# Router logits of an attention + FFN + mixture kernel: x tiles as the stationary operand instead of the gate

## The chip, the cores and the metric

The kernel runs on one NeuronCore of a Trainium2 chip, in one launch. The metric is the device time of one execution in microseconds. Three executions of the kernel before took 2273.41, 2275.58 and 2281.95 us; the median is 2275.58 us.

TensorE (PE in the profile; PEld is its weight load) does the matrix products: a stationary operand (`lhsT`) is loaded, then the columns of a moving operand (`rhs`) are streamed past it, and the result lands in PSUM. VectorE is DVE, ScalarE is ACT, GpSimd is POOL. SyncE (SP) issues all DMAs of this kernel.

## What is computed

Three layers follow one another on 4 sequences of 576 tokens, 2304 tokens in all, width 512: causal attention with a decay, a gated FFN, and a mixture of 8 experts whose weights per token come from a router. The change is in the router:

```python
def _moe2_ref(x, w_gate, w1, w2):
    logits = x @ w_gate                      # 2304 x 512 by 512 x 8
    logits = logits - logits.max()
    P = np.exp(logits)
    for _ in range(8):                       # rows and columns normalised in turn
        P /= P.sum(1, keepdims=True) + 1e-09
        P /= P.sum(0, keepdims=True) + 1e-09
        P *= N / E
    for e in range(E):
        out += P[:, e:e+1] * (np.maximum(x @ w1[e], 0) @ w2[e])
```

## The kernel before, in words

**Precision.** Products are made from split operands: every fp32 value is cast to fp32r (`hi`, on ACT) and the rest `x - hi` is formed on POOL (`rest`, L142). Most products take three matmuls: hi·hi, hi·lo and lo·hi.

**Stages.** `merge` interleaves two streams of steps by their costs: the attention of sequence b (`attn_unit(b)`) with the FFN of sequence b-1 (`moe_unit(b-1)`). The FFN leaves its result `x` of 512 x 576 with the *features* on the 128 partitions (four chunks k) and the tokens along the row. Sequence 3's FFN has no attention beside it (L519). Then come two phases of 32 slices (256 hidden columns of one expert): `wload` fetches and splits the weights, `eup` makes the hidden values of two sequences with seven products in place of eight (Strassen, L578), `edown` multiplies by w2 for nine tiles of 128 tokens and adds into `acc`. Expert 0 of phase 0 is added unweighted, since the router's weights are not there yet; from expert 1 on, each tile is scaled by `lg[:, t, e]` (L626, L630).

**The router.** At the end of each sequence's FFN, `finish` (L433) writes x to DRAM, and for each half of 288 tokens and each pair i of feature chunks casts x to `f` (ACT, L443, POOL for the rest), and runs four matmuls (L447) with the gate stationary and 288 tokens moving. The gate tile `gw` holds, for each feature chunk, 8 columns of hi, 8 of lo and 112 of zeros, so each product has 128 output rows, of which 16 count. ACT copies these 16 rows (L451) and a DMA writes them to `lgd` in DRAM (L452). In phase 0, after the first slice, `gate` (L637) reads `lgd` back in five pieces, transposes each tile of 16 x 128 on TensorE (L645), and DVE adds the lo part to the hi part into `lg`, with tokens on the partitions (L648, L649). `balance` (L651) then makes the exponentials and eight rounds of row and column sums on DVE, with one small matmul a round (L674).

**What sets the order.** The Tile framework puts instructions on each engine in an order that its scheduler chooses, and adds the semaphore waits; each engine then runs its own list strictly in that order. PSUM has eight banks: `ps_m` has three tiles of one bank each, for the FFN's products and for `pl`; when it is closed (L520), its banks go to later pools, `ps_y` among them, in which `edown` works.

Of the kernel before, what the change touches and what calls it, by code (L numbers as in the profile page):

```python
# [8 lines left out]
F32 = mybir.dt.float32  # L9
F32R = mybir.dt.float32r  # L10
# [4 lines left out]
ALU = mybir.AluOpType  # L15
# [18 lines left out]
def attention_two_ffns(ctx: ExitStack, tc: tile.TileContext, qkT, vt, f, wf, g2, w1, w2, out):  # L34
    nc = tc.nc
    B, H, D, _, S = qkT.shape
    NT, DM = out.shape
    NPC = wf.shape[0]
    DFF = NPC * 256 // 3
    E, _, F2 = w1.shape  # L40
    P = 128
    KD = DM // P
    NTILE = NT // P
# [30 lines left out]
    gs = const.tile([P, KD, E], F32, name="gs")  # L74
    nc.sync.dma_start(out=gs, in_=g2.rearrange("(k p) e -> p k e", p=P))

    gw = const.tile([P, KD, P], F32R, name="gw")
    nc.vector.memset(gw.bitcast(F32), 0.0)
    nc.vector.tensor_copy(out=gw[:, :, 0:E], in_=gs)
    nc.vector.tensor_tensor(out=gw[:, :, E:2 * E], in0=gs, in1=gw[:, :, 0:E].bitcast(F32), op=ALU.subtract)  # L80

# [1 line left out]
    HB = S // 2  # L83
    NF = 7
    xd = [dram.tile([P, KD, S], F32, name=f"xd{b}") for b in range(B)]
    lgd = dram.tile([2 * E, NT], F32, name="lgd")

# [292 lines left out]
    def moe_unit(b, get=fetch, ready=None):  # L382
# [50 lines left out]
        def finish():  # L433

            x = xa["x"]
            nc.sync.dma_start(out=xd[b], in_=x)
            for j in range(2):
                tk = slice(j * HB, (j + 1) * HB)
                pl = ps_m.tile([P, 512], F32, tag="m", name="pl")
                for i in range(2):  # L440
                    t = frm.tile([P, 2, 2, HB], F32R, tag="f", name="f")
                    src = x[:, 2 * i:2 * i + 2, tk]
                    nc.scalar.copy(out=t[:, 0], in_=src)  # L443
                    rest(t[:, 1], src, t[:, 0])
                    ops = [(hl, k) for k in range(2) for hl in range(2)]
                    for n, (hl, k) in enumerate(ops):
                        nc.tensor.matmul(  # L447
                            out=pl[:, 0:HB], lhsT=gw[:, 2 * i + k], rhs=t[:, hl, k],
                            start=(i == 0 and n == 0), stop=(i == 1 and n == len(ops) - 1))
                ls = frm.tile([P, HB], F32, tag="ls", name="ls", bufs=1)  # L450
                nc.scalar.copy(out=ls[0:2 * E], in_=pl[0:2 * E, 0:HB])  # L451
                nc.sync.dma_start(out=lgd[:, b * S + j * HB:b * S + (j + 1) * HB], in_=ls[0:2 * E])  # L452

        nb = len(blocks)

# [176 lines left out]
            if e == E - 1 and s == F2 // FS - 1:  # L632
                nc.sync.dma_start(out=out[t * P:(t + 1) * P, :], in_=a)

    lg = ep.tile([P, NTILE, E], F32, name="lg")

    def gate():  # L637
        for t0 in range(0, NT, 512):
            n = min(512, NT - t0)
            ls = sk.tile([P, 512], F32, tag="ls", name="ls")[0:2 * E]  # L640
            nc.sync.dma_start(out=ls[:, 0:n], in_=lgd[:, t0:t0 + n])
            pz = ps_z.tile([P, 512], F32, tag="z", name="pz")
            nt = n // P
            for t in range(nt):
                nc.tensor.transpose(pz[:, 2 * t * E:2 * (t + 1) * E], ls[:, t * P:(t + 1) * P], ident[0:2 * E, 0:2 * E])  # L645
            lt = lg[:, t0 // P:t0 // P + nt, :]
            parts = pz[:, 0:2 * nt * E].rearrange("p (t h e) -> p t h e", t=nt, h=2)
            nc.vector.tensor_copy(out=lt, in_=parts[:, :, 1])  # L648
            nc.vector.tensor_tensor(out=lt, in0=parts[:, :, 0], in1=lt, op=ALU.add)  # L649

    def balance():  # L651
        mx = sk.tile([P, 1], F32, tag="mx", name="mx")
        nc.vector.tensor_reduce(out=mx, in_=lg.rearrange("p t e -> p (t e)"), op=ALU.max, axis=mybir.AxisListType.X)
# [30 lines left out]
    for i in range(len(slices)):  # L684
        wload(i + 1)
        for g in range(NB):
            eup(i, g)
            if i + 1 == len(slices) // NPH:
                merge(xload(NB + g))
            if g == 0 and i:  # L690
                edown(i - 1, range(split, TP))
            if g == 1:
                edown(i, range(0, split))
        if i == 0:
            gate()
            balance()
    edown(len(slices) - 1, range(split, TP))

# [30 lines left out]
```

## Time and profile before

| | |
|---|---|
| median of 3 executions | 2275.58 us (2273.41 to 2281.95) |
| the profiled execution | 2276.13 us |
| its span, first to last instruction | 2274.3 us |
| PE busy | 2224.4 us, 98% of the span |
| PEld busy | 2019.3 us, 89% |
| DVE busy | 1688.4 us, 74% |
| POOL, ACT busy | 884.6 us (39%), 849.7 us (37%) |
| granted TensorE clock, mean | 0.995 |

Busy time of an engine is the time in which at least one of its instructions has a record open. Matmuls overlap: a record of 0.29 us can be followed by the next start 0.13 us later, so the pace is read from starts and not from the length of records.

### The profile page before, as it was taken

Reading aid. Unit: us, or ns where it says so; the run is one execution under the profiler, and the core shown is the slowest. Engines: PE = TensorE matmul, PEld = TensorE weight load, DVE = VectorE, ACT = ScalarE, POOL = GpSimd, SP = SyncE. Lnnn points to the kernel's source line nnn. Section 1 sums busy time; section 2 is a strip of 40 time slices with the busy share of each in tenths; the row PEclk is TensorE's granted clock in tenths of the full one; section 3 lists DMA queues with packets and bytes.
Section 4 is the critical chain, followed back from the end, with each engine's and each line's share of the span. In section 5 each row is a group of like instructions: output and inputs, shape, how many; then the busy total and the mean of one; then the engine's idle time right before and its main releaser. Section 6 shows DMA issues by size and latency. Waiting matters only on the chain.

```text
span 2274.3 us, 36164 instructions
## 1 busy us (share of the span) xinstructions
PE 2224.4 (98%) x13881; PEld 2019.3 (89%) x13881; DVE 1688.4 (74%) x3385; ACT 849.7 (37%) x1936; POOL 884.6 (39%) x668
## 2 busy tenths in 40 slices
PE   7899999999999999999999999989999999999999
PEld 5698899999999898988988989979889898898897
DVE  6678854544535798888878888886888787887876
ACT  7766754454322433322323222333232232322321
POOL 6869863342423432323323233353233232332320
PEclk9999999999999999999999999999999999999999
DMA  8666664454644211111111111121111111111101
GB/s 246 196 213 217 214 229 159 163 171 148 232 160 153 70 46 40 47 47 38 56 38 47 47 39 56 48 90 51 43 43 51 38 56 38 47 47 38 56 29 51
DMA packets 95469, 215.97 MB, mean 95 GB/s; under 512 B 10000, under 2 KB 52288, under 8 KB 83264
## 3 DMA queue, kind: packets, MB, share of 16 engines
q1 hardware_dynamic: 95296, 213.66, 29.1%
q8 instruction: 109, 1.79, 0.3%
q14 instruction: 64, 0.52, 0.1%
HBM read 185.02 MB, written 28.61 MB: 94 GB/s over the span
## 4 chain that ended last, share of the span: by engine, by line
PE 85%; DVE 6%; DMA 4%; ACT 2%; issue 1%; POOL 1%; SPq 0%; DVEq 0%; ACTq 0%; POOLq 0%
PE py L150 39%; PE pa L578 29%; PE pm L150 11%; DMA st<-wf 2%; PE ps_o L340 2%; PE ps_t L309 1%; DVE al L593 1%; DMA xst<-xd 1%; PE ps_s L272 1%; PE ps_s L268 1%; DVE np L274 1%; DVE xt L508 1%; PE ps_o L332 1%; DVE c L587 0%; DMA qk<-qkT 0%
## 5 line engine op out<-in xcount | busy, mean ns | idle before, releaser
L578 PE MATMUL pa<-xf,w1h 128*128 128x288 f32 x3584 | 749.2, 295 | 7.0 <-DVE c L587 6.6
L578 PEld LDWEIGHTS pa<-xf,w1h 128*128 128x128 f32 x3584 | 597.7, 188 | 45.9 <-DVE c L587 8.4
L630 DVE SCALAR_TENSOR_TENSOR acc<-py,lg,acc 128x512 f32<-128x512 f32 x531 | 395.1, 744 | 241.2 <-PE py L150 240.9
L578 PE MATMUL pa<-xf,w1l 128*128 128x288 f32 x1792 | 527.4, 295 | 0.0
L142 POOL TENSOR_TENSOR w2l<-w,w2h 128x1024 fp32r<-128x1024 f32 x64 | 154.8, 2420 | 825.2 <-ACT w2h L554 825.0
L150 PE MATMUL py<-w2h,ah 128*128 128x512 f32 x1152 | 454.1, 394 | 4.2 <-DVE acc L623 2.5
L150 PE MATMUL py<-w2l,ah 128*128 128x512 f32 x1152 | 454.1, 394 | 0.0
L150 PE MATMUL py<-w2h,al 128*128 128x512 f32 x1152 | 453.2, 393 | 0.0
L593 DVE SCALAR_TENSOR_TENSOR al<-c,ah 128x288 fp32r<-128x288 f32 x512 | 426.7, 860 | 7.4 <-ACT ah L592 6.7
L592 ACT ACTIVATE ah<-c 128x288 fp32r<-128x288 f32 x512 | 208.1, 443 | 590.9 <-PE py L150 318.9
L578 PEld LDWEIGHTS pa<-xf,w1l 128*128 128x128 f32 x1792 | 337.0, 188 | 10.5
L150 PE MATMUL pm<-xh,w 128*128 128x288 f32 x1536 | 326.5, 298 | 3.4 <-DVE xa L431 1.9
L150 PEld LDWEIGHTS py<-w2h,al 128*128 128x128 f32 x1152 | 216.3, 188 | 49.9
L150 PEld LDWEIGHTS pm<-xh,w 128*128 128x128 f32 x1536 | 252.0, 188 | 6.2 <-DVE xa L431 2.5
L150 PEld LDWEIGHTS py<-w2h,ah 128*128 128x128 f32 x1152 | 216.4, 188 | 33.3 <-DVE acc L623 2.9
L150 PEld LDWEIGHTS py<-w2l,ah 128*128 128x128 f32 x1152 | 216.3, 188 | 26.0
L142 POOL TENSOR_TENSOR w1l<-w,w1h 128x256 fp32r<-128x256 f32 x192 | 162.0, 870 | 179.1 <-ACT w1h L550 179.1
L150 PE MATMUL pm<-xl,w 128*128 128x288 f32 x768 | 226.4, 295 | 2.6 <-POOL xl L142 2.6
L598 ACT COPY m<-pa 128x288 f32<-128x288 f32 x128 | 50.2, 392 | 436.0 <-PE pa L578 433.6
L150 PE MATMUL py<-ah,w 128*128 128x288 f32 x768 | 174.6, 299 | 3.5 <-DVE xa L431 1.6
L142 POOL TENSOR_TENSOR al<-th,ah 128x288 fp32r<-128x288 f32 x96 | 82.0, 854 | 201.8 <-ACT ah L415 201.8
L142 POOL TENSOR_TENSOR w1l<-sm,w1h 128x1024 fp32r<-128x1024 f32 x64 | 154.6, 2415 | 2.5 <-ACT w1h L550 2.5
(138 smaller groups left out, 3102.6 us busy)
## 6 DMA issues: line engine op xcount, KB each, us to landing
w<-w SPq DMA_DIRECT2D x128, 512.0 KB, 3.6
w<-wsplit SPq DMA_DIRECT2D x54, 1024.0 KB, 5.8
qk<-qkT SPq DMA_DIRECT2D x64, 288.0 KB, 5.5
st<-wf SPq DMA_DIRECT2D x18, 1024.0 KB, 8.4
wsplit<-w SPq DMA_DIRECT2D x18, 1024.0 KB, 5.0
cb<-cumd SPq DMA_DIRECT2D x31, 288.0 KB, 3.3
xd<-xa SPq DMA_DIRECT2D x4, 1152.0 KB
xst<-xd SPq DMA_DIRECT2D x8, 576.0 KB, 6.1
```

What stands on the lines that cost most here:

```text
L142: (eng or nc.gpsimd).tensor_tensor(out=out, in0=src, in1=hi.bitcast(F32), op=ALU.subtract)
L150: nc.tensor.matmul(out=ps, lhsT=a, rhs=b, start=(i == 0), stop=(i == n - 1))
L268: nc.tensor.matmul(out=ps[:, 0:w], lhsT=a[:, qs:qs + P], rhs=kh[:, c0:c0 + w], start=True, stop=False)
L272: nc.tensor.matmul(out=ps[:, 0:w], lhsT=a[:, qs:qs + P], rhs=kl[:, c0:c0 + w], start=False, stop=True)
L274: nc.vector.tensor_tensor_reduce(out=pt[r0:P, c0:c0 + use], in0=ps[r0:P, 0:use], in1=cb[r0:P, c0:c0 + use], scale=-SCALE, scalar=prev, op0 ...
L309: nc.tensor.transpose(pv[:, j, :], pt[r0:P, k0:k0 + P], ident[r0:P, r0:P])
L340: nc.tensor.matmul(out=po[:, c0:w], lhsT=vs[:, j, e].rearrange("p a d -> p (a d)"), rhs=pts[rng][part][:, j, c0:w], start=(i == 0), stop=( ...
L578: nc.tensor.matmul(out=ps, lhsT=w[:, MW[m - 1], k], rhs=x[:, m - 1, hl, k], start=(n == 0), stop=(n == len(ops) - 1))
L592: nc.scalar.activation(out=ah[:, f, tk], in_=src, func=AF.Relu)
L593: nc.vector.scalar_tensor_tensor(out=al[:, f, tk], in0=src, scalar=0.0, in1=ah[:, f, tk].bitcast(F32), op0=ALU.max, op1=ALU.subtract)
L598: nc.scalar.copy(out=m1, in_=p1)
L630: nc.vector.scalar_tensor_tensor(out=a, in0=py, scalar=lg[:, t, e:e + 1], in1=a, op0=ALU.mult, op1=ALU.add)
```

## The change

The operands of the logits' matmuls change places. A tile of x, [128 features x up to 128 tokens], is now stationary, and the gate's 16 columns (8 hi, 8 lo) move; the result has tokens on the partitions. The gate tile loses its zeros. A sequence of 576 tokens covers 4.5 tiles of 128 tokens, so `finish` works in two parts of 256 and 320 tokens (sequences 0 and 2) or 320 and 256 (1 and 3), in five tiles a sequence, one of them of 64 tokens; each takes eight matmuls. All tiles of a part write their 16 columns into one PSUM tile `pl`, at column offsets of their own. DVE copies the lo part to `lg` and adds the hi part (two operations a tile); where the tile begins in the middle of a partition range (r is 64), the sum goes to `half` first and ACT copies it. `lgd`, `gate` with its reads and transposes, and the copies to `ls` go. `lg` moves to the pool that lives all along.

```diff
-    gw = const.tile([P, KD, P], F32R, name="gw")
-    nc.vector.memset(gw.bitcast(F32), 0.0)
+    gw = const.tile([P, KD, 2 * E], F32R, name="gw")
...
-    lgd = dram.tile([2 * E, NT], F32, name="lgd")
+    lg = const.tile([P, NTILE, E], F32, name="lg")
...
-            for j in range(2):
-                tk = slice(j * HB, (j + 1) * HB)
-                pl = ps_m.tile([P, 512], F32, tag="m", name="pl")
+            t0 = b * S
+            mid = (t0 + 320) // P * P - t0
+            for c0, c1 in ((0, mid), (mid, S)):
+                ts = []
                 for i in range(2):
-                    t = frm.tile([P, 2, 2, HB], F32R, tag="f", name="f")
-                    src = x[:, 2 * i:2 * i + 2, tk]
+                    t = frm.tile([P, 2, 2, 320], F32R, tag="f", name="f")[:, :, :, 0:c1 - c0]
+                    src = x[:, 2 * i:2 * i + 2, c0:c1]
                     nc.scalar.copy(out=t[:, 0], in_=src)
                     rest(t[:, 1], src, t[:, 0])
-                    ops = [(hl, k) for k in range(2) for hl in range(2)]
-                    for n, (hl, k) in enumerate(ops):
-                        nc.tensor.matmul(
-                            out=pl[:, 0:HB], lhsT=gw[:, 2 * i + k], rhs=t[:, hl, k],
-                            start=(i == 0 and n == 0), stop=(i == 1 and n == len(ops) - 1))
-                ls = frm.tile([P, HB], F32, tag="ls", name="ls", bufs=1)
-                nc.scalar.copy(out=ls[0:2 * E], in_=pl[0:2 * E, 0:HB])
-                nc.sync.dma_start(out=lgd[:, b * S + j * HB:b * S + (j + 1) * HB], in_=ls[0:2 * E])
+                    ts.append(t)
+                pl = ps_m.tile([P, 512], F32, tag="m", name="pl")
+                c = c0
+                while c < c1:
+                    n, r = divmod(t0 + c, P)
+                    w = min(P - r, c1 - c)
+                    po = pl[0:w, 2 * E * (n % 8):2 * E * (n % 8 + 1)]
+                    ops = [(i, k, hl) for i in range(2) for k in range(2) for hl in range(2)]
+                    for m, (i, k, hl) in enumerate(ops):
+                        nc.tensor.matmul(
+                            out=po, lhsT=ts[i][:, hl, k, c - c0:c - c0 + w], rhs=gw[:, 2 * i + k, 0:2 * E],
+                            start=(m == 0), stop=(m == len(ops) - 1))
+                    to = frm.tile([P, E], F32, tag="half", name="half", bufs=1)[0:w] if r else lg[0:w, n]
+                    nc.vector.tensor_copy(out=to, in_=po[:, E:2 * E])
+                    nc.vector.tensor_tensor(out=to, in0=po[:, 0:E], in1=to, op=ALU.add)
+                    if r:
+                        nc.scalar.copy(out=lg[r:r + w, n], in_=to)
+                    c += w
...
-    lg = ep.tile([P, NTILE, E], F32, name="lg")
-
-    def gate():
...
         if i == 0:
-            gate()
             balance()
```

The order of the instructions moves with it. The first place is PE's list at the end of sequence 3's FFN, in the kernel before. `pl` is the logits' product, `f` the split x, `pa` a product of `eup`, `w1h` and `w1l` its split weights; `x2` stands for two alike, and what an instruction waits for stands in brackets.

```order
L447 MATMUL pl<-f,gw 128x288 [waits DVE_49,Activation_49]
L447 MATMUL pl<-f,gw 128x288 [waits Pool_49]
L447 MATMUL pl<-f,gw 128x288 x2
L447 MATMUL pl<-f,gw 128x288 [waits Activation_49]
L447 MATMUL pl<-f,gw 128x288 [waits Pool_49]
L447 MATMUL pl<-f,gw 128x288 x2
L578 MATMUL pa<-xf,w1h 128x288 [waits Activation_49]
L578 MATMUL pa<-xf,w1h 128x288
```

The eight matmuls of the first half stand together; those of the second half follow in pieces of 1, 4 and 3, with 12 `pa` matmuls ahead of them and 18 and 11 between them.

The same place on PE with the change, from the second tile of sequence 3 on (the first, of 64 tokens, stands before it in pieces of 1, 4 and 3 among `pa` matmuls):

```order
L456 MATMUL pl<-gw,f 128x16 [waits DVE_49]
L456 MATMUL pl<-gw,f 128x16 x7
L456 MATMUL pl<-gw,f 128x16 [waits DVE_49]
L456 MATMUL pl<-gw,f 128x16 x7
L456 MATMUL pl<-gw,f 128x16 [waits Activation_49]
L456 MATMUL pl<-gw,f 128x16 [waits Pool_49]
L456 MATMUL pl<-gw,f 128x16 x2
L456 MATMUL pl<-gw,f 128x16 [waits Activation_49]
L456 MATMUL pl<-gw,f 128x16 [waits Pool_49]
L456 MATMUL pl<-gw,f 128x16 x2
L590 MATMUL pa<-xf,w1h 128x288 [waits Activation_49]
L590 MATMUL pa<-xf,w1h 128x288
```

Four of the five tiles of sequence 3 now stand almost together: two tiles of the first part, then one of the second, two `pa` matmuls, and the last tile (which also begins with a wait for DVE). The 24 `pa` matmuls that stand right before these rows end the first slice; the `pa` after them belong to the second.

The second place is ACT's list there, with the change (`m` and `ah` are copies and results of `eup`; the `f` of 640 columns are those of the first part, 128x2x256 those of the second):

```order
L444 CAST f<-xa 128x640 [waits DVE_49]
L610 COPY m_9241<-pa 128x288 [waits PE_49,Pool_49]
L444 CAST f<-xa 128x640 [waits DVE_49]
L604 ACTIVATE ah<-c 128x288 [waits DMAHW4_49,DMAHW5_49,DMAHW1_49,DMAHW7_49,DMAHW0_49,DVE_49]
L604 ACTIVATE ah<-c 128x288 [waits DVE_49]
L610 COPY m_9314<-pa 128x288 [waits PE_49]
L604 ACTIVATE ah<-c 128x288 [waits DVE_49] x3
L463 COPY lg<-half 64x8 [waits DVE_49]
L604 ACTIVATE ah<-c 128x288 [waits DVE_49] x3
L444 CAST f<-xa 128x2x256 [waits PE_49,Pool_49] x2
L562 CAST w1h<-w_9209 128x256 x3
```

The two casts of the second part wait for PE's last matmul on the first part, since there are two buffers `f`; the cast of the next slice's weights (`w1h`) stands behind them. In the kernel before, all four casts of `f` stood ahead of the first `ah` of `eup`, with one copy to `m` and the copy to `ls` between them.

## Rows read from the trace of the kernel before

**Rows 1.** Page, part 1: busy us of each engine, share of the span, instructions.

```profile
PE 2224.4 (98%) x13881; PEld 2019.3 (89%) x13881; DVE 1688.4 (74%) x3385; ACT 849.7 (37%) x1936; POOL 884.6 (39%) x668
```

**Rows 2.** Windows: stretch and its length, then busy us (instructions), clock, DMA share, GB/s.

```profile
200.00:300.00 100.00, 93.19 (x647) 84.55 (x647) 87.34 (x189) 70.87 (x166) 88.55 (x68) 0.97 0.68 220
300.00:340.00 40.00, 39.72 (x301) 37.99 (x300) 19.78 (x56) 23.09 (x58) 19.86 (x19) 1.00 0.72 245
```

**Rows 3.** Page, part 4: the chain that ended last, shares of the span by engine.

```profile
PE 85%; DVE 6%; DMA 4%; ACT 2%; issue 1%; POOL 1%; SPq 0%; DVEq 0%; ACTq 0%; POOLq 0%
```

**Rows 4.** Timeline of PE at 740 us: start, length of the group, line, tile, count.

```profile
740.13 1.23 PE L447 MATMUL pl<-f,gw 128*128 128x288 f32 x8
741.19 0.42 PE L578 MATMUL pa<-xf,w1h 128*128 128x288 f32 x2
```

**Rows 5.** Lines by form, PE: all logits matmuls and all transposes; busy us, mean ns.

```profile
L447 PE MATMUL pl<-f,gw 128*128 128x288 f32 x64 | 11.4, 301 | 0.5 <-ACT f L443 0.5
L645 PE MATMUL pz<-ident,ls 16*128 16x16 f32 x18 | 2.0, 214 | 0.0
```

**Rows 6.** Timeline of PE at 753 us: one group of four transposes and its neighbours.

```profile
753.09 0.39 PE L150 MATMUL py<-w2l,ah 128*128 128x512 f32 x1
753.32 0.40 PE L150 MATMUL py<-w2h,al 128*128 128x512 f32 x1
753.65 0.42 PE L645 MATMUL pz<-ident,ls 16*128 16x16 f32 x4
754.00 0.53 PE L578 MATMUL pa<-xf,w1h 128*128 128x288 f32 x2
```

**Rows 7.** Timeline of PE at 795 us: two matmuls with 8 moving columns among others.

```profile
795.77 0.28 PE L674 MATMUL pz<-cs,ones 128*128 128x8 f32 x2
795.91 0.51 PE L578 MATMUL pa<-xf,w1h 128*128 128x288 f32 x2
796.26 0.30 PE L578 MATMUL pa<-xf,w1l 128*128 128x288 f32 x1
```

**Rows 8.** Lines by form, PEld: loads of 128, 128 and 10 columns; busy us, mean ns.

```profile
L447 PEld LDWEIGHTS pl<-f,gw 128*128 128x128 f32 x64 | 9.4, 188 | 0.8 <-ACT f L443 0.7
...
L674 PEld LDWEIGHTS pz<-cs,ones 128*128 128x128 f32 x16 | 2.8, 188 | 0.3
...
L288 PEld LDWEIGHTS ps_r<-ident,rc 128*10 128x10 f32 x16 | 1.4, 89 | 1.1 <-DVE pt L318 0.5 <-DVE pt L313 0.3 <-issue 0.2
```

**Rows 9.** Tile f: ns min/median/max of the cast and of the rest, 576 columns each.

```profile
L443 ACT CAST f<-xa x16: 660/672/677, 304.0 to 741.8; 128x576 fp32r<-128x576 f32 x16
L142 POOL TENSOR_TENSOR f<-xa,f x16: 1414/1432/1651, 304.8 to 743.0; 128x576 fp32r<-128x576 f32 x16
```

**Rows 10.** Timelines of ACT and of POOL: a cast of f, and the rest behind it.

```profile
740.90 0.67 ACT L443 CAST f<-xa 128x576 fp32r<-128x576 f32 x1
...
741.66 3.03 POOL L142 TENSOR_TENSOR f<-xa,f 128x576 fp32r<-128x576 f32 x2 [1.85 <-ACT f L443]
```

**Rows 11.** Timeline of DVE at 757 us: the copy and the addition of the logits.

```profile
757.73 0.18 DVE L648 COPY lg<-pz 128x32 f32<-128x32 f32 x1
757.94 0.19 DVE L649 TENSOR_TENSOR lg<-pz,lg 128x32 f32<-128x32 f32 x1
```

**Rows 12.** Waits of PE from 740 to 900 us: in total, times, longest.

```profile
PE py L150 <- DVE acc L623: 2.5, 1, 2.5
PE pa L578 <- DVE c L587: 0.6, 1, 0.6
PE py L150 <- ACT acc L621: 0.5, 1, 0.5
```

**Rows 13.** Tile ls: who waited for its copies, writes and reads; us, times.

```profile
ACT ls L451: 3.9, 2
...
PE pm L150: 0.3, 1
```

**Rows 14.** Lines by form, DVE, 740 to 760 us: the slowest kind; mean ns.

```profile
L593 DVE SCALAR_TENSOR_TENSOR al<-c,ah 128x288 fp32r<-128x288 f32 x8 | 8.1, 1030 | 0.6 <-ACT ah L592 0.6
```

More of the change, by code (lines that the diff above doesn't have):

```diff
@@ L633, in edown @@
                 nc.sync.dma_start(out=out[t * P:(t + 1) * P, :], in_=a)
-    lg = ep.tile([P, NTILE, E], F32, name="lg")
-    def gate():
[L638 to L649, printed above, removed]
     def balance():
```

## The prediction

> **What bounds the kernel now.** I read the page's shares first. PE is busy 98% of the span [rows 1], but that is the time with a matmul's record open, so the windows by stage come next: from 200 to 300 us PE lacks 6.8 us of 100, from 300 to 340 us 0.3 of 40, at a granted clock of 1.00 [rows 2]. The change's first instruction on PE stands at about 311 us. The chain that ended last runs through PE for 85% of the span [rows 3]. So from there on TensorE is the bound, and its time is the sum of the paces of its matmuls: what is added to that sum is added to the run. The other engines count only where they make PE wait. The list of waits from 740 to 900 us, which holds the last logits, the transposes and the eight balancing rounds, shows 3.6 us in three waits, 2.5 of them one wait for a DVE eviction [rows 12]. The DMAs that go were waited for by ACT, 3.9 us, and hardly by PE, 0.3 us behind the copy to `ls` [rows 13]: DRAM's round trip was hidden, and taking it away gives next to nothing.
>
> **What goes.** Eight logits matmuls start at 740.13 us and the next other matmul at 741.19 [rows 4]: 1.06 us for eight, 0.133 us each. The zeros in the gate cost nothing there, since 288 columns are streamed in any case. 64 of them [rows 5] are 8.5 us. A group of four transposes: the 512-column matmul that starts at 753.32 us would by its neighbour's pace (753.09 to 753.32) let the next one start at 753.55; that one starts at 754.00 [rows 6]. So a group costs 0.45 us, and 18 transposes [rows 5] in four groups of four and one of two cost about 2.1 us. Eight copies to `ls` on ACT, eight writes and five reads on SP's queue, the memset of `gw` and ten DVE operations of 0.18 and 0.19 us [rows 11] go beside PE and count as nothing: PE's own work covers them. Together 10.6 us go.
>
> **What comes on PE.** Five tiles a sequence with eight matmuls each are 160 matmuls: 128 with a stationary tile of 128 tokens and 32 with one of 64. They stream only 16 columns, so the weight load sets their pace. The trace has a near relative: two matmuls with full 128 x 128 weights and 8 columns start at 795.77 us; with the two ordinary ones behind them (0.133 each) they reach to 796.26 [rows 7]. 0.49 less 0.27 leaves 0.22 for two, 0.112 us each. Their loads have the same length as those of the logits, 188 ns [rows 8], so 128 of them make 14.3 us. A load of 64 columns is not in the trace. A load of 10 columns takes 89 ns where 128 take 188 [rows 8]: on that line 64 columns take 54 ns less than 128, a pace of 0.058 us, so 32 make 1.9 us; the bounds are a load as short as that of 10 columns, 0.013, and one as long as that of 128, 0.112, which make 0.4 to 3.6 us. I take 1.9, since 64 lies about half way between the two rows. 16.2 us come, 10.6 go: **PE's work grows by 5.6 us.**
>
> The Trainium skill (TensorE: Matmul & The Clock Gate, section LDWEIGHTS) says that a load takes its number of columns divided by 1.2, in ns, whatever the contraction. That is 107 ns for 128 columns, near the 0.112 us of the row, and 53 ns for 64; the sum by it would be 15.4 us in place of 16.2.
>
> **What comes as waits.** Each tile's first matmul waits for DVE to have read the tile before it out of the same PSUM tile `pl`; the order shows this wait on every tile but the first of each part, 12 in all. Its price: a small matmul's record of 0.21 us [rows 5], DVE's copy and addition from 757.73 to 758.13, 0.40 us [rows 11], and a hop between engines at either end of about 0.08 us, as from the end of ACT's cast at 741.57 us to POOL's start at 741.66 [rows 10]: 0.77 us. In nine of the twelve the order has 11 or more other matmuls in between (1.5 us), which cover it. The others: in sequence 2 three matmuls (0.40 us) cover part of one, leaving 0.37; in sequence 3 one is bare, 0.77, and one has two `pa` matmuls (0.27), leaving 0.50. 1.6 us.
>
> The last is a bubble in sequence 3. There the second part's two casts wait for the first part's last matmul, and nothing of PE's stands between. From that matmul: 0.21 us for its record, 0.08, a cast of 512 columns at 512/576 of 0.672 us, 0.60 [rows 9], 0.08, two rests on POOL at 512/576 of 1.432 us, 2.54 in all [rows 9], 0.08: 3.6 us, of which PE fills five small matmuls, 0.6. **3.0 us idle**, that the kernel before didn't have, because `pa` matmuls of the first slice stood between its pieces. At the starts of the other second parts 5 to 16 matmuls stand in the gap, where before it was 1 in sequence 2, and I count nothing.
>
> 20 pairs of small DVE operations come, 15 pairs more than went, about 6 us spread from 311 us on; two copies come on ACT. They stand beside PE. The eight rounds of `balance` are the same instructions, begun some 60 matmuls earlier in PE's list; their DVE work still meets the evictions, and I leave that stretch as it is.
>
> **Sum.** 5.6 + 1.6 + 3.0 = 10.2 us. The profiled execution took 2276.13 us, so it would take 2286.3; the median of the runs is 0.55 us lower, so I predict 2286 us, 0.45% more. A measurement of this kernel tells about 0.5% from no change, 11.4 us, so the limits are 2264.2 and 2287.0 us: the forecast lies just inside, and its own spread of some 5 us (1.7 us up and 1.5 down for the narrow loads, 0.77 for each handover more or less, 3.6 us of waits that the order can move) crosses the upper one.
>
> **Rivals.** *The handover becomes a queue.* DVE takes its list in order, and a copy out of `pl` that the order places well can stand behind a slow neighbour: beside POOL's work, the `al` operations took 1.03 us on average at 740 to 760 us [rows 14]. With one of these ahead of the copy and one ahead of the addition a handover takes 0.77 + 2.06 = 2.83 us and sticks out of the smallest cover, 1.5 us, by 1.3. At half of that for each of the nine covered ones it is 6 us more: 2292; at the whole, 12 us: 2298. It decides where the handover with its neighbours exceeds the cover. For it: the order gives PE nothing to pass by a waiting matmul, and `pl` holds one of three `ps_m` banks for a whole part, which leaves two to the FFN. Against it: before the change PE hardly waits from 311 us on. The Trainium skill (PSUM — Partial Sum Buffer, section "PSUM bank collisions raise a hardware error") speaks against the change here: two engines must be kept apart by semaphores per bank and quarter of the partitions, not per address, so that tiles in one bank must hand over one by one. The waits in the order agree.
>
> *Loads that don't overlap, or double.* If the narrow matmuls run one after another at the full 188 ns of a load, or if each is issued as two as the 8-column ones were (16 records for eight rounds [rows 8]), the 160 take 28 to 32 us: 2298 to 2302. The pace of rows 7 speaks against the first, and the single records of the 288-column matmuls of the same type [rows 5] against the second.
>
> *The earlier balance gives back its waits.* With `lg` complete at the end of `finish`, the rounds fall into the first slice, whose evictions ACT takes. If all 3.6 us of waits [rows 12] go and the transposes' gaps with them, it is 2282.
>
> *Faster by more than 0.5%* would need 22 us off the sum. There is not so much idle time on PE after 311 us, so this would be a mechanism that I don't see.
>
> **Chances.** Forecast, 2281 to 2291: 0.55, of which 0.33 below 2287.0 and 0.22 above. Balance gives back: 0.18, no change. Queue: 0.19, slower. Loads: 0.05, slower. Something unseen and faster: 0.03. So faster 0.03, same 0.51, slower 0.46. The range reaches down to 2276 (3.6 us of waits gained, and the bubble and the handovers filled by a luckier meeting of engines) and up to 2298, which takes in the queue and leaves out most of the loads.
>
> **What would show it.** Right: the narrow matmuls appear as 160 records, eight in about 0.9 us; PE's idle time before them names DVE's L461 a few times and POOL's rest of `f` for some 3 us near 745 us, once. Right as to the DMAs: SP's queue is shorter and nothing starts earlier. Wrong: eight narrow matmuls in 0.5 us or in 1.5 us; waits of PE for DVE at most of the twelve handovers; a clock below 1.00 around the bubble, which the kernel before shows only ahead of 300 us [rows 2]; or a span that shrinks between 760 and 880 us by more than 4 us.

## The result and the profile after

The changed kernel takes 2290.33 us, the median of six runs (2288.70 to 2296.07), against 2276.86 us of the kernel before in the same set (2273.41 to 2281.95). The ratio of the means is 1.0063, with a 95% interval of 1.0045 to 1.0081: slower, by about as much as a measurement here can tell from no change. 2286 had been forecast, with a range of 2276 to 2298. The profiled execution took 2288.70 us, its span is 2286.9 us.

Page, part 1, of the changed kernel: busy us, share of the span, instructions.

```profile
PE 2236.5 (98%) x13959; PEld 2032.8 (89%) x13959; DVE 1688.6 (74%) x3414; ACT 848.7 (37%) x1930; POOL 881.4 (39%) x668
```

Against [rows 1] PE's busy time has grown by 12.1 us and that of its loads by 13.5; PE's share is 98% as before. Such a total doesn't say whether PE had more work or took longer for it. The windows do. The changed kernel, columns as in rows 2: length, then busy us of PE, PEld, DVE, ACT and POOL, clock, DMA share, GB/s.

```profile
600.00:620.00 20.00, 19.43 (x148) 19.25 (x146) 8.76 (x20) 4.98 (x11) 6.08 (x7) 1.00 0.55 194
620.00:625.00 5.00, 3.09 (x14) 2.73 (x14) 2.85 (x7) 2.35 (x4) 3.42 (x3) 0.67 1.00 391
625.00:630.00 5.00, 5.00 (x28) 5.00 (x28) 0.45 (x1) 0.68 (x2) 4.37 (x3) 0.65 0.08 31
630.00:640.00 10.00, 10.00 (x80) 10.00 (x80) 2.85 (x9) 2.12 (x5) 2.11 (x3) 1.00 0.05 12
740.00:760.00 20.00, 18.34 (x141) 17.90 (x140) 14.17 (x38) 8.05 (x19) 5.36 (x5) 1.00 0.15 60
760.00:765.00 5.00, 3.67 (x18) 3.45 (x18) 0.33 (x2) 2.74 (x5) 5.00 (x6) 0.66 0.00 0
765.00:770.00 5.00, 5.00 (x23) 4.79 (x23) 3.27 (x6) 1.42 (x4) 5.00 (x4) 0.65 0.35 110
...
800.00:900.00 100.00, 100.00 (x596) 90.54 (x595) 88.20 (x201) 35.24 (x73) 28.92 (x20) 1.00 0.15 47
```

Two things stand here that the sum of the prediction has not. At the ends of sequence 2 (620 us) and sequence 3 (760 us) PE lacks busy time, and in each of these places the granted clock falls to the half level (1.2 of 2.4 GHz). From 625 to 630 us PE is busy all the time and gets through 28 matmuls, where the kernel before gets through 40. The loss is (1 - clock) x 5 us in each window: 1.65 + 1.75 = 3.4 us at the end of sequence 2, 1.70 + 1.75 = 3.4 us at that of sequence 3. The kernel before has a clock of 1.00 in both. And from 800 to 900 us PE has no idle time left; the waits of [rows 12] are gone.

The end of sequence 2 on PE's timeline, with the idle time before a row and what ended it in brackets:

```profile
618.20 0.95 PE L456 MATMUL pl<-gw,f 128*128 128x16 f32 x8
619.73 0.40 PE L590 MATMUL pa<-xf,w1h 128*128 128x288 f32 x1 [0.57 <-ACT xf L524]
621.21 0.40 PE L590 MATMUL pa<-xf,w1h 128*128 128x288 f32 x1 [1.08 <-POOL xf L142]
621.44 0.29 PE L590 MATMUL pa<-xf,w1l 128*128 128x288 f32 x1
622.57 1.88 PE L456 MATMUL pl<-gw,f 128*128 128x16 f32 x8 [0.83 <-DVE lg L461]
624.30 1.31 PE L590 MATMUL pa<-xf,w1h 128*128 128x288 f32 x4
```

Eight narrow matmuls take 0.95 us from the first start to the last end, at the pace that was forecast. The second tile starts 4.37 us after the first; of the three `pa` in between, two wait for their own `xf`. PE idles 2.48 us in three gaps. The granted clock is 1.00 up to 621.7 us and 0.50 from there, so the fall stands behind the first two gaps, and the third, of 0.83 us, lies within it. The second tile takes 1.88 us, at half the clock. DVE's timeline there shows what the tile waited for:

```profile
620.11 1.35 DVE L520 TENSOR_TENSOR xt<-xst,xt 128x288 f32<-128x288 f32 x1
621.39 0.15 DVE L460 COPY lg<-pl 128x8 f32<-128x8 f32 x1
621.50 0.94 DVE L520 TENSOR_TENSOR xt<-xt,xst 128x288 f32<-128x288 f32 x1
622.36 0.15 DVE L461 TENSOR_TENSOR lg<-pl,lg 128x8 f32<-128x8 f32 x1
```

Copy and addition take 0.15 us each, but one stands behind a subtraction of `xload` of 1.35 us and the other behind one of 0.94. The first tile was done at about 619.2 us, `pl` is free at 622.5. The end of sequence 3 on PE:

```profile
756.58 0.95 PE L456 MATMUL pl<-gw,f 128*128 128x16 f32 x8
757.99 1.06 PE L456 MATMUL pl<-gw,f 128*128 128x16 f32 x8 [0.46 <-DVE lg L461]
759.37 0.28 PE L456 MATMUL pl<-gw,f 128*128 128x16 f32 x1 [0.32 <-ACT f L444]
760.71 0.61 PE L456 MATMUL pl<-gw,f 128*128 128x16 f32 x4 [1.07 <-POOL f L142]
761.94 0.81 PE L456 MATMUL pl<-gw,f 128*128 128x16 f32 x3 [0.62 <-POOL f L142]
762.61 0.83 PE L590 MATMUL pa<-xf,w1h 128*128 128x288 f32 x2
763.23 1.85 PE L456 MATMUL pl<-gw,f 128*128 128x16 f32 x8
```

One bare handover (0.46) and the bubble in three pieces (2.01); the clock falls at 761.7 us, within the last piece. The last tile, behind two `pa`, shows no idle time.

### The profile page after: what moved, and what is told of

Its sections match the earlier page's. It is cut to its first block, busy times and chain, and to the rows that moved or that the text cites. A ratio compares the mean times of both kernels' runs of the same rounds, so it can differ in the third digit from the quotient of the medians.

```text
span 2286.9 us, 36321 instructions
## 1 busy us (share of the span) xinstructions
PE 2236.5 (98%) x13959; PEld 2032.8 (89%) x13959; DVE 1688.6 (74%) x3414; ACT 848.7 (37%) x1930; POOL 881.4 (39%) x668
## 4 chain that ended last, share of the span: by engine, by line
PE 86%; DVE 5%; DMA 4%; ACT 2%; POOL 1%; issue 1%; SPq 0%; POOLq 0%; DVEq 0%; ACTq 0%
PE py L150 39%; PE pa L590 31%; PE pm L150 11%; DMA st<-wf 2%; PE ps_o L340 2%; PE ps_t L309 1%; PE ps_s L272 1%; DMA xst<-xd 1%; PE ps_s L268 1%; DVE xt L520 1%; DVE al L605 1%; DMA rd<-rt 1%; PE ps_o L332 1%; DVE np L274 1%; PE pl L456 1%
## 5 line engine op out<-in xcount | busy, mean ns | idle before, releaser
L605 DVE SCALAR_TENSOR_TENSOR al<-c,ah 128x288 fp32r<-128x288 f32 x512 | 417.8, 843 | 13.1 <-ACT ah L604 11.8
```

Of the source, the lines that this page charges most:

```text
L605: nc.vector.scalar_tensor_tensor(out=al[:, f, tk], in0=src, scalar=0.0, in1=ah[:, f, tk].bitcast(F32), op0=ALU.max, op1=ALU.subtract)
```

## An account that every trace can be put through

The first some 310 us differ from execution to execution and from kernel to kernel: the first logits matmul starts between 308.0 and 316.6 us in the fourteen traces, at 311.8 and 312.2 in the two of the kernel before. So single profiles are compared from that matmul to the end. That time is taken apart in three: *clock*, the sum of (1 - granted clock) x 5 us over windows of 5 us; *waits*, over all matmuls, what the distance from one start to the next has above the median distance behind matmuls of the same tiles and shape, counted where it is over 0.3 us; and *work*, the rest. Where PE idles at the half level, the same time stands in *clock* and in *waits* (about 0.4 us at 622 us of the changed kernel, half of the gap of 0.83), and *work* is too small by as much. The labels are those of the experiments below. The column "ends" is the part of the clock's loss that lies at the ends of sequences 2 and 3 (590 to 660 and 740 to 790 us).

| kernel | first logits | from there to the end | clock | ends | waits | work |
|---|---|---|---|---|---|---|
| before | 311.8 | 1962.5 | 0.0 | 0.0 | 14.9 | 1947.6 |
| before, control | 312.2 | 1963.0 | 3.4 | 0.0 | 12.7 | 1946.9 |
| after | 308.0 | 1978.9 | 8.5 | 6.8 | 16.5 | 1953.9 |
| after, control | 309.7 | 1979.9 | 8.5 | 6.8 | 18.2 | 1953.1 |
| e_cols128 | 310.5 | 1978.6 | 8.5 | 5.1 | 18.2 | 1951.9 |
| e_banks | 316.6 | 1975.3 | 6.8 | 5.1 | 14.3 | 1954.2 |
| e_f3 | 313.9 | 1976.1 | 6.8 | 3.4 | 14.2 | 1955.1 |
| e_wide | 309.7 | 1977.9 | 5.1 | 3.4 | 24.4 | 1948.4 |
| e_order | 311.2 | 1984.5 | 10.2 | 8.5 | 20.4 | 1953.8 |
| e_late | 311.5 | 1983.6 | 12.0 | 8.6 | 18.8 | 1952.9 |
| e_all | 316.2 | 1976.9 | 5.1 | 3.4 | 16.6 | 1955.2 |
| e_tile | 313.6 | 1970.7 | 3.4 | 1.7 | 14.3 | 1953.0 |
| e_tile2 | 312.3 | 1990.3 | 6.8 | 1.7 | 14.7 | 1968.8 |
| e_split | 311.3 | 1960.5 | 1.7 | 0.0 | 11.3 | 1947.5 |

With the mean of the two traces of either kernel the change adds 16.65 us from the first logits on: 6.25 of work, 6.8 of clock, 3.55 of waits. The waits by place: 2.1 more at the end of sequence 2, 3.45 more at that of sequence 3, 3.3 less from 790 to 900 us, 1.3 more elsewhere. A start that was 3.15 us earlier takes the spans to 13.5 apart, and the medians are 13.5 apart.

Each experiment below has executions of the kernel before in its own set, with medians of 2276.43, 2277.60 or 2279.01 us, and its ratio is taken against those; medians of different sets are compared only roughly.

The theory to be tried: the change costs PE some 6 us of work, and the rest is idle time at the ends of two sequences with the falls of the clock behind it, less some 4 us that the earlier balance gives back.

## Experiments: the controls

**e_before**, the kernel before once more.

> The kernel before, unchanged, as a control: what of the differences between two profiles is chance. Theory (the falls of the granted clock behind 300 us belong to the change): the profile shows no fall at the ends of sequences 2 and 3, and none at about 1520 us. Rival (such falls come and go in any execution): one or more of them here too, with a span some 2 to 3 us longer for each. The first 300 us may differ by some 4 us either way.

The rival holds for single falls: this trace has two, neither at the ends of the sequences. Its price of 2 to 3 us a fall doesn't show in the span, which is 0.9 us longer in all: by the table two falls cost 3.4 us, and 2.9 us of shorter waits and work stand against them. The best pair of rows in the study is the wait of [rows 12] in the two executions of this one kernel. First the profile of before, PE's timeline, then its window; then the same two of the control:

```profile
855.71 0.50 PE L150 MATMUL py<-w2h,ah 128*128 128x512 f32 x1 [2.47 <-DVE acc L623]
```

```profile
855.00:860.00 5.00, 4.29 (x23) 3.77 (x24) 4.93 (x15) 0.45 (x1) 0.03 (x1) 1.00 0.35 105
```

```profile
855.23 0.50 PE L150 MATMUL py<-w2h,ah 128*128 128x512 f32 x1 [2.46 <-DVE acc L623]
```

```profile
855.00:860.00 5.00, 4.78 (x17) 4.13 (x18) 4.90 (x16) 0.45 (x1) 0.00 (x0) 0.66 0.36 105
```

The same wait, to 0.01 us, was followed by the full clock in one execution and by the half level in the other, which by the account cost 1.7 us more. A wait of some 2.5 us thus has a price of its own and a second one that is paid or not. The other fall, near 1500 us, stands in 13 of the 14 traces of the study; the one without it is the profile on which the prediction was made.

**e_after**, the changed kernel once more.

> The changed kernel, unchanged, as a control for its own profile. Theory: the idle time at the ends of sequences 2 and 3 is the same to 0.3 us, the clock falls at both places or at one of them, and the span differs by what the first 300 us and the falls differ.

2291.38 us. The waits at both places are there again (1.1, 0.8 and 0.7 us at the end of sequence 2 by the list of waits), and so are both falls, 6.8 us. At these two places together the loss is no chance of one execution: the 11 traces of the ten kernels that form the logits in place lose 1.7 to 8.6 us there, the three of before and e_split nothing.

## Experiments: what makes the clock fall

**e_cols128** pads the gate to 128 columns, so each narrow matmul streams 128 columns in place of 16.

```diff
-    gw = const.tile([P, KD, 2 * E], F32R, name="gw")
+    gw = const.tile([P, KD, P], F32R, name="gw")
+    nc.vector.memset(gw.bitcast(F32), 0.0)
...
-                    po = pl[0:w, 2 * E * (n % 8):2 * E * (n % 8 + 1)]
+                    po = pl[0:w, o:o + P]
+                    o += P
...
-                            out=po, lhsT=ts[i][:, hl, k, c - c0:c - c0 + w], rhs=gw[:, 2 * i + k, 0:2 * E],
+                            out=po, lhsT=ts[i][:, hl, k, c - c0:c - c0 + w], rhs=gw[:, 2 * i + k],
```

> The changed kernel, but the gate is padded with zeros to 128 columns, so that each narrow matmul streams 128 columns in place of 16; the result is the same. Same matmuls, waits and order. Theory (the granted clock falls behind stretches in which TensorE only loads weights and streams 16 columns): no fall to the half level at 621 and at 761 us, so about 2 x 3.4 us less: 2282 to 2285 us. Rival (the idle gaps at the ends of sequences 2 and 3 alone bring the clock down): both falls stay, 2288 to 2292 us. Rival (the streams cost PE more than the loads): eight matmuls in over 1.0 us and a longer run, 2292 or more.

2292.90 us, ratio 1.0068 (1.0051 to 1.0086). For these two places my first theory falls. Windows of this kernel:

```profile
625.00:630.00 5.00, 5.00 (x28) 4.89 (x27) 0.45 (x3) 1.72 (x4) 4.86 (x3) 0.66 0.39 166
...
760.00:765.00 5.00, 3.55 (x15) 2.98 (x14) 0.67 (x4) 3.72 (x7) 4.63 (x6) 0.65 0.00 0
765.00:770.00 5.00, 5.00 (x26) 4.87 (x27) 2.16 (x5) 1.42 (x4) 5.00 (x3) 0.67 0.32 105
```

The clock falls in the same two places, though PE streams eight times the columns; the waits there stayed. At the end of sequence 2 the fall cost 1.7 us in place of 3.4. It did so in e_f3 below too, whose edit leaves that place alone, so one trace can't put this down to the padding. A stream of 16 columns is thus not needed for a fall. That idle time is needed is not shown by this, and e_tile2 below speaks against it. The work is the same as with 16 columns (1951.9 against 1953.5), so a stream of 128 columns hides behind the load too.

## Experiments: the waits, one at a time

**e_banks** gives each token tile a PSUM tile of its own.

```diff
-                    po = pl[0:w, 2 * E * (n % 8):2 * E * (n % 8 + 1)]
+                    po = ps_m.tile([P, 512], F32, tag="m", name="pl")[0:w, 0:2 * E]
```

> The changed kernel, but each token tile has a PSUM tile of its own in place of a share in one, so no tile waits for DVE's reading of the one before it. Theory (the handover is a small part of the loss): the wait of 0.6 us between two narrow tiles of sequence 3 and the one of 0.8 us in sequence 2 go, 1 to 2 us less: 2288 to 2290 us, and both falls of the clock stay, as the waits for f stay. Rival (the handovers are the loss): 6 us or more less, 2284 us or below.

2290.85 us, 1.0060 (1.0041 to 1.0080): no gain in the median, 4.1 us less from the first logits on (1975.3 against 1979.4), while this profile started late (316.6). At the end of sequence 3 the waits of narrow matmuls and the fall are gone; but the order had moved with the edit (3 to 22 `pa` now stand between groups of tiles there), so this isn't the handover alone. At the end of sequence 2 a wait for DVE and the fall stayed; the fall was longer and cost 5.1 us in place of 3.4. List of waits from 600 to 660 us (us in total, times, longest):

```profile
PE pl L455 <- DVE lg L459: 0.9, 1, 0.9
PE pa L589 <- ACT xf L523: 0.5, 1, 0.5
PE pa L589 <- POOL xf L142: 0.3, 1, 0.3
```

**e_f3** gives sequence 3's second part two `f` buffers of its own.

```diff
-                    t = frm.tile([P, 2, 2, 320], F32R, tag="f", name="f")[:, :, :, 0:c1 - c0]
+                    t = (fx[0] if b == 3 and c0 else frm).tile([P, 2, 2, 320], F32R, tag="f", name="f")[:, :, :, 0:c1 - c0]
...
+    fx.append(m_ctx.enter_context(pool2("frx", 2)))
```

> The changed kernel, but the second part of sequence 3 has two f buffers of its own, in space that the attention pools have left, so that its casts don't wait for the first part's matmuls. Theory (the bubble of sequence 3 is the waits for f, 2.4 us, and the fall of the clock behind it, 3.4 us, follows from it): 2.5 us less if the clock still falls, 6 us less if it doesn't: 2284 to 2288 us; sequence 2 and its fall of the clock stay as they are. Rival (the wait moves to the ls or half buffers or to the handover): within 1 us of the changed kernel.

2291.61 us, 1.0065 (1.0045 to 1.0085). In the trace the bubble is gone, as these waits from 740 to 790 us show, and 3.3 us with it (1976.1 against 1979.4), near the lower of the two expected gains; the median doesn't show it. The clock still fell at the end of sequence 3, at 769 us, behind the wait of 0.9 us below and three tiles of narrow matmuls, for 1.7 us in place of 3.4. At the end of sequence 2, which the edit leaves alone, it lost 1.7 us as well, so the length of a fall varies by itself.

```profile
PE pa L592 <- DVE c L601: 0.9, 1, 0.9
PE pl L457 <- ACT f L445: 0.2, 1, 0.2
```

**e_order** holds the first `pa` behind FFN products of sequence 3 in PE's issue order (`hold[1]` is the last `pm` of that sequence's second `up`).

```diff
-            eup(i, g)
+            with tc.issue_after(hold[1].ins) if i == 0 else ExitStack():
+                eup(i, g)
```

> The changed kernel, but the first eup products (pa) are held behind FFN products (pm) of sequence 3 in the issue order, so that no pa stands between the narrow tiles at the end of sequence 2. Theory (2.5 us of idle time there come from pa matmuls placed ahead of their xf, and the fall of the clock, 3.4 us, follows from the idle time): the waits for xf and the fall at 621 us go, 4 to 6 us less than the changed kernel: 2284 to 2287 us. Rival (the narrow matmuls bring the clock down): fall and time stay within 2 us. Rival (the wait moves to the handover or to the f of the second part): idle time there of the same size and no gain.

2297.91 us, 1.0089 (1.0075 to 1.0102): slower, and the third theory holds for the end of sequence 2. Without `pa` the order puts the first two tiles side by side, and the handover stands bare. PE's timeline at the end of sequence 2:

```profile
621.71 0.95 PE L460 MATMUL pl<-gw,f 128*128 128x16 f32 x8
626.02 1.53 PE L460 MATMUL pl<-gw,f 128*128 128x16 f32 x8 [3.36 <-DVE lg L465]
```

and DVE's:

```profile
623.58 1.35 DVE L524 TENSOR_TENSOR xt<-xst,xt 128x288 f32<-128x288 f32 x1
624.85 0.15 DVE L464 COPY lg<-pl 128x8 f32<-128x8 f32 x1
624.96 0.93 DVE L524 TENSOR_TENSOR xt<-xt,xst 128x288 f32<-128x288 f32 x1
625.82 0.15 DVE L465 TENSOR_TENSOR lg<-pl,lg 128x8 f32<-128x8 f32 x1
```

So the `pa` matmuls' waits for `xf` were not the cause in the changed kernel. They lay in the shadow of this one: 3.36 us bare, 2.48 with three `pa` in it.

That isn't what made this kernel slower, though. From the first logits on it is 5.1 us longer than the changed kernel (1984.5 against 1979.4), and only 0.8 of that are waits at the end of sequence 2. Another 1.7 us is a longer fall at the end of sequence 3, and 3.1 us are waits between 790 and 900 us, which the changed kernel hasn't. The longest of them:

```profile
PE pz L674 <- DVE cs L671: 1.5, 1, 1.5
```

This is a wait in the rounds of `balance`, which the edit left at its early place.

**e_all** joins the edits of e_order and e_f3, without others.

> Both repairs together: pa held behind pm as in the second kernel of this batch, and the second part of sequence 3 with f buffers of its own. Theory (what is left is PE's extra work of 5.6 us less what the early balance gives back): no idle time above 1 us at the ends of the sequences, no fall of the clock there, 2278 to 2282 us. Rival (the loss is spread over all four sequences): 2286 us or more, without falls of the clock.

2291.15 us, 1.0055 (1.0039 to 1.0070). Sequence 3 loses no clock; sequence 2 has the bare handover again (3.1 us) and its 3.4 us of clock. Neither the theory's 2278 to 2282 us nor the rival, which had no falls, came true. Two repairs that leave the handover to DVE aren't enough.

**e_late** puts `balance` one slice later.

```diff
-        if i == 0:
+        if i == 1:
             balance()
```

> The changed kernel, but balance stands one slice later in the program, near where it stood before. Theory (the early balance gave back some 4 us between 800 and 900 us): idle time of PE of some 3 us returns there, 2 to 4 us more: 2292 to 2295 us. Rival (the waits of the kernel before were chance or came from the DRAM reads and transposes): no wait returns, the time stays within 1 us of the changed kernel.

2294.23 us, 1.0077 (1.0062 to 1.0091). One wait of PE between 790 and 900 us is back, where the changed kernel has none:

```profile
PE pz L670 <- DVE cs L667: 1.5, 1, 1.5
```

with a fall of 1.7 us behind it: 3.2 us. The median is 3.9 us longer than that of the changed kernel, and the trace from the first logits on 4.2, in which a longer fall at the end of sequence 3 stands too (1.7 us). The intervals overlap, so the times alone don't show it. The rows fit the theory, as does the control with its wait of 2.46 us at the old place. But e_order has the same wait of 1.5 us with `balance` at the early place, so that the place alone decides is not shown.

## Experiments: the matmuls themselves

**e_wide** keeps the gate stationary, copies the logits to SBUF and transposes them inside each sequence: no DRAM, no narrow matmuls.

```diff
+                            out=pl[:, 0:nn], lhsT=gw[:, 2 * i + k], rhs=t[:, hl, k],
...
+                nc.scalar.copy(out=ls, in_=pl[0:2 * E, 0:nn])
...
+                    nc.tensor.transpose(po, ls[:, c - c0:c - c0 + w], ident[0:2 * E, 0:2 * E])
```

> One part of the change alone: no DRAM, no gate at the end, balance early, but the logits are formed as before with gate's columns stationary and 256 or 320 tokens moving, copied to SBUF and transposed (20 transposes) inside each sequence. Theory (the loss comes from the narrow matmuls and what stands around them; the DRAM round trip was hidden and its removal gives nothing; the earlier balance gives back some 4 us): 2272 to 2278 us, and no fall of the clock behind 300 us. Rival (removing the DRAM and the late gate is worth something that the narrow matmuls hide): below 2270 us. Rival (the place of the work at the sequences' ends is what costs, not its form): 2283 us or more, with the clock falling at the same places.

2295.81 us, 1.0077 (1.0057 to 1.0097): no faster than the change, 18 us above the theory's range, and as its second rival had it the clock falls at the same places. Its work is that of before (1948.4), the falls at the ends cost 3.4, and the waits are 24.4 us. From 300 to 600 us:

```profile
PE ps_s L268 <- POOL qkh L142: 2.6, 1, 2.6
PE ps_s L268 <- DVE mn L274: 1.7, 4, 0.7
PE py L150 <- DVE th L413: 1.3, 1, 1.3
```

Logits work put between two stages was paid here in waits of PE, though its form was the old one. It need not be: e_tile and e_banks, with 14.3 us of waits, have about as much as the kernel before. That DRAM's removal alone gains nothing was expected and isn't contradicted, but this kernel has too many waits of its own to show it.

**e_tile** makes `f` per token tile in three small buffers, with one `pl` for a sequence and `pa` held as in e_order; 18 or more other matmuls stand between any two tiles.

```diff
-                    t = frm.tile([P, 2, 2, 320], F32R, tag="f", name="f")[:, :, :, 0:c1 - c0]
+                t = frm.tile([P, 2, KD, P], F32R, tag="f", name="f", bufs=3)[:, :, :, 0:w]
+                src = x[:, :, c:c + w]
...
+                    nc.tensor.matmul(out=po, lhsT=t[:, hl, k], rhs=gw[:, k], start=(m == 0), stop=(m == len(ops) - 1))
```

> The changed kernel, but f is made per token tile (128 or 64 tokens, all four chunks of x in one cast and one rest) in three smaller buffers, and pa is held behind pm as before; so 18 or more other matmuls stand between any two narrow tiles. Theory (PE's added work is about 6 us, the early balance gives some 4 back, and the rest of the loss is idle time at the ends of sequences 2 and 3 with the falls of the clock behind it): no wait above 0.5 us there, no fall of the clock at those places, 2278 to 2284 us, 7 to 10 us less than the changed kernel. Rival (the narrow matmuls cost the time wherever they stand): 2288 us or more.

2287.24 us, 1.0039 (1.0026 to 1.0051). From the first logits on it is 8.7 us shorter than the changed kernel (1970.7 against 1979.4), within the 7 to 10 expected. The median is only 3.1 shorter and misses the expected range by 3; the profile's first logits start 4.8 us later than those of the changed kernel (313.6 against 308.9 on average), which is most of the difference. The handover has shrunk to 0.3 us, but waits above 0.5 us are left. From 600 to 660 us:

```profile
PE pm L152 <- DVE th L415: 0.9, 1, 0.9
PE py L152 <- DVE th L415: 0.6, 1, 0.6
PE pl L454 <- DVE lg L457: 0.3, 1, 0.3
```

and from 740 to 790 us:

```profile
PE pa L586 <- DVE c L595: 2.3, 2, 1.5
```

These are waits for DVE in work that was always there. The clock lost 1.7 us behind those of sequence 2, and nothing behind those of sequence 3, the longest of 1.5 us. The work stays at 1953.0: that part doesn't go away.

**e_tile2** does every narrow matmul of e_tile twice.

```diff
-                for m, (k, hl) in enumerate(ops):
+                for m, (k, hl) in list(enumerate(ops)) * 2:
```

> The kernel with f per token tile, with every narrow matmul done twice (the second pass overwrites the first, the result is the same): 160 more of them at the paces of 0.112 and 0.058 us. Theory (PE's work alone sets what they cost where nothing waits): 16 us more than the kernel with f per token tile, 14 to 18. Rival (they hide in part beside waits): under 10 us more. Rival (narrow streams bring the clock down): over 20 us more, with falls of the clock at the ends of the sequences.

2300.78 us, 1.0098 (1.0082 to 1.0115): 13.5 us more in the median, just under the 14 to 18 expected, and 15.8 us more work in the trace (1968.8 against 1953.0). The forecast for 160 narrow matmuls was 16.2. They hide nowhere.

At the ends of sequences 2 and 3 the clock loses no more than with half as many (1.7). But the whole trace has two falls more than e_tile, and they stand at the ends of sequences 0 and 1, at 331 and 491 us, where no other trace of the study has one. Ahead of the second, three tiles of 16 narrow matmuls start at 479.44, 484.56 and 489.55 us, and from 475 to 500 us the list of waits is empty:

```profile
485.00:490.00 5.00, 5.00 (x40) 4.64 (x40) 1.63 (x7) 1.80 (x5) 0.80 (x1) 1.00 0.09 25
490.00:495.00 5.00, 5.00 (x30) 5.00 (x30) 1.82 (x7) 0.94 (x4) 0.00 (x0) 0.66 0.00 0
```

PE is busy all the time, and the clock falls. So idle time isn't needed for a fall either, and the rival that narrow matmuls bring the clock down holds here in its mechanism, though not in its 20 us. A wait without narrow matmuls (e_before), waits with padded ones (e_cols128) and narrow ones without waits (here) each had a fall behind them. The two falls of the changed kernel have both ahead of them, and which of the two brought them is not shown.

**e_split** is the kernel before, with the reads and transposes of sequences 0 to 2 (13 of the 18 tiles) traced beside sequence 3's FFN, so that `balance` begins earlier.

```diff
+    early = [(1.0, lambda t0=t0: gate(t0, 512 if t0 < 1536 else 128, frm, ps_m, "m")) for t0 in (0, 512, 1024, 1536)]
-    merge(moe_unit(3), xload(0) + xload(1))
+    merge(moe_unit(3), xload(0) + xload(1) + early)
...
-            gate()
+            gate(1664, 512, sk, ps_z, "z")
+            gate(2176, 128, sk, ps_z, "z")
```

> The kernel before, with lg in the pool that lives all along and the gate's reads and transposes of sequences 0 to 2 traced beside sequence 3's FFN, so that only five tiles are left for the end and balance stands earlier; matmuls, DRAM and the number of transposes as before. Theory (of the change, only the earlier balance gains, some 4 us, and it needs no narrow matmuls): 2271 to 2277 us, without the wait of 2.6 us at about 853 us. Rival (the transposes placed earlier bring new waits): 2280 us or more.

2273.93 us, the median of 11 runs (2271.09 to 2278.15), 0.9987 (0.9977 to 0.9996): the only version faster than before, by 0.13%. Its windows:

```profile
600.00:640.00 40.00, 39.50 (x297) 39.16 (x296) 14.80 (x31) 12.66 (x27) 16.51 (x14) 1.00 0.61 217
740.00:800.00 60.00, 59.54 (x366) 53.68 (x365) 50.47 (x117) 25.45 (x56) 23.84 (x17) 1.00 0.19 66
800.00:900.00 100.00, 100.00 (x593) 90.31 (x592) 87.01 (x195) 36.72 (x76) 33.04 (x24) 1.00 0.15 48
```

PE's idle time between 800 and 900 us is gone as in the changed kernel (before: 96.94 busy), the clock is whole at all three places, and the work is that of before.

## Why the prediction was right and where it was wrong

**PE's work: right.** 5.6 us were forecast, 6.25 measured as the difference of the work. 16.2 us for the 160 narrow matmuls were forecast, 15.8 measured by doubling them. The two paces, 0.112 us read from a pair of matmuls that did something else [rows 7] and 0.058 us interpolated between two load lengths [rows 8], are the median distances of two starts in the trace: 0.112 for 128 tokens, 0.058 for 64. By the rule of the Trainium skill (TensorE: Matmul & The Clock Gate, section LDWEIGHTS) that a load takes its columns divided by 1.2, in ns, the 160 are estimated at 15.4 us; the measured 15.8 agrees to 0.4 us.

**The DMAs: right as far as shown.** e_split keeps all the reads and writes and is faster than before, so their going isn't what an earlier `balance` needs. That no other transfer starts earlier without them is not shown by a row.

**The bubble of sequence 3: right in place and kind, smaller in size.** 3.0 us for the waits for `f` were forecast; the trace has 0.32 + 1.07 + 0.62 = 2.01 of idle time. A part of the difference is that the first cast did not wait for the first part's last matmul. The first four matmuls of a tile read one buffer `f` and the last four the other, and the cast starts while the tile of 757.99 to 759.05 us still runs:

```profile
758.70 1.14 ACT L444 CAST f<-xa 128x512 fp32r<-128x512 f32 x2 [0.75 <-PE pl L456]
```

By starts, as the forecast counted, the whole end of sequence 3 lost 3.45 us more than in the kernel before, against 4.3 for the bubble and two handovers.

**Handovers: right where bare, wrong in sequence 2.** In sequence 3 a bare one was priced at 0.77 us, and PE idled 0.46; the one behind two `pa`, priced at 0.50, cost no idle time. In sequence 2 the term was that three matmuls "cover part of one, leaving 0.37"; PE idled 2.48. The price had DVE's two operations back to back. On the chip each stood behind a subtraction of `xload`. That is the rival "the handover becomes a queue", at one of twelve handovers and not at nine; its bound for a bare one, 2.83 us, is near the 3.36 of e_order.

**Balance: "I leave that stretch as it is" was wrong.** The waits went from 3.3 us to nothing, as the third rival had it; e_split has the gain without the rest of the change. e_late brings part of them back, but so does e_order with `balance` left early, so the gain is not sure to follow from the place.

**The clock: the step that failed.** The whole sum was made at a clock of 1.00, as from 300 us on in the only profile there was. A fall was named as a sign against the prediction and had no price. It cost 6.8 us at the two places, 3.4 at each. The idle time of sequence 3 and the narrow matmuls were both in the forecast, so a price for a fall belonged there, as a chance. Which of them brought the clock down stays open: the runs show falls behind either alone.

So 2286.0 against 2290.33 comes from errors of either sign: from the first logits on +10.2 were forecast and +16.65 measured, which is 6.8 for the clock and 0.65 more work, less about 1 us of waits (3.55 in all against the 4.6 of handovers and bubble). The earlier start, which nothing in the forecast foresaw, took 3 us back; that the number came so near is in part luck. PE's added work, which is what one sees in the diff, is 6 of 16 us. The chance of the three outcomes was fair: the ratio's interval still holds 1.005.

## What to carry to other kernels

Price an idle gap of TensorE, where it is the bottleneck, twice: its length, and the stretch at the half clock that may follow it; two executions of one kernel show the same gap with and without it, so one clean profile proves nothing. Tiles of narrow matmuls close together deserve the same caution: one trace has a fall behind three of them without a gap. A handover between engines costs what stands ahead of it in the other engine's list at that place, and a short operation in a busy list is not short. Before work is moved into the seam between two stages, look for what the move brings besides: here the one gain came with an earlier `balance`, which the old form of the matmuls could have as well.

## What was not expected of the hardware

Padding the moving operand from 16 to 128 columns left the pace of the narrow matmuls as it was (0.112 us), and the clock fell in the same two places. The clock fell to the half level at 621.7 us of the changed kernel behind gaps of 0.57 and 1.08 us, and at 491 us of e_tile2 behind none, while it stayed whole in the profile of before behind single gaps of 2.47 us at 855 us and 3.18 at 1512. What decides between the two was not tried.
